# Attention and a SoLU feed-forward layer in one kernel: larger local units, two jobs moved to GpSimd, one to TensorE, and a new instruction order

## The chip, the cores and the metric

The kernel runs on one core of one Trainium2 chip. Five engines matter: TensorE (PE, matmuls), VectorE (DVE), ScalarE (ACT), GpSimd (POOL) and SyncE (SP, which here only issues DMAs). Each executes its own instructions in the order in which they stand in the program, and waits on semaphores for the others. The time is the device time of one execution in microseconds; the lower the better. The kernel before took 507.43 us (median of 3 runs, 505.02 to 507.56).

## The reference

```python
# q, k, v: (8, 8, 576, 64); heads 0-3 see the last 32 keys, heads 4-7 every 32nd key
scores = scale * np.matmul(q, k.transpose(0, 1, 3, 2))
mask_local = (rel >= 0) & (rel < 32)
mask_strided = (rel >= 0) & (pos[None, :] % 32 == pos[:, None] % 32)
attn = softmax(np.where(masks, scores, -1e9))       # eps 1e-9 in the sum
x = np.matmul(attn, v) -> (4608, 512)               # 8 batches of 576 tokens, 8 heads * 64
# feed-forward, on all 4608 tokens
h = x @ w_in                                        # 512 x 1024
solu = h * softmax(h)
ln = (solu - mean) / np.sqrt(var + 1e-6) * g_ln     # over the 1024
out = ln @ w_out                                    # 1024 x 512
```

The input weights arrive as 64-bit floats and are decoded on the chip.

## The kernel before, in words

**Attention.** The scores that a mask keeps are computed in small blocks, and blocks are handled in *units*. `unit(n)` takes unit n; each of the 8 batches has five (`UNITS`): two strided ones (6 and 5 blocks of 54 queries and 54 keys for each of 4 heads) and three local ones (3 blocks each of 64 queries and 96 keys). So units 0 to 4 belong to batch 0 and unit 7 is the first local one of batch 1. A unit runs this chain: the mask is put into the PSUM tile `s_ps` (the first six units by four matmuls of a unit matrix on TensorE, L369; from unit 6 on by a copy on ScalarE, L361, called the *seed*), TensorE adds the fp32 products of queries and keys (L374), VectorE takes the maxima (L380) and subtracts them (L390), ScalarE does the exponentials (L392), VectorE the sums (L393), VectorE two small instructions for the reciprocals (L397, L398), GpSimd the product with them (L401), ScalarE the fp16 high part (L409), VectorE the low part (L410), a DMA transposes both into `pt` (L412), TensorE multiplies with v (L432 strided, L442 local), and ScalarE and VectorE copy the result from PSUM as high and low part (L461, L462) into the rings `xl` and `xs`. In the units of `BY_BLOCK` the exponentials are taken block by block straight from PSUM with their sums (L385). There is one `s_ps`, so a unit's scores can only start when the unit before it has left it.

**v.** For each batch ScalarE squares the raw v (L303, output thrown away into `junk`), a power-of-two scale comes of it, and ScalarE and VectorE split v in high and low parts (L325, L326).

**Feed-forward.** `ff(n)` handles 128 tokens; there are 36. `g1` is 24 matmuls of 128x128 by 128x512 (three fp16 products for each of 4 x 2 pieces, L505 to L507) into two of three PSUM banks `h_ps`; maxima (L511), exponentials (L515), products (L517), centring (L521), squares (L522), the norms on GpSimd (L525 to L555), high and low part of the result (L562, L563), a DMA transpose (L566), and `g2`, again 24 such matmuls (L575 to L577), into `o_ps`; ScalarE scales and stores (L583).

**Weights.** `decode` turns 64-bit floats into 32-bit ones: ScalarE makes the upper bits (L603), VectorE shifts the low word (L606) and joins it (L607). w_in (four pieces) and w_out (four pieces) both pass it, in `prep_w` and `prep_o`. `prep_w` then forms the sum of squares with TensorE (`gram`, L620), and splits w_in (L628 on ScalarE, L629 on VectorE). `prep_o` forms the squares of w_out with ScalarE (L639, eight times) and splits w_out (L651, L652).

**Order.** Every step is entered in a plan with its engine, a planned duration, what it reads and what it writes. `ORDER`, a table of step numbers, gives the order in which they are emitted, and so the order on every engine and on the DMA queue of SyncE. `lock=True` in a step tells the search of that table that a VectorE instruction with two SBUF inputs and a GpSimd instruction exclude each other.

The step that the change replaces in `decode`, and the two reciprocal steps, as they stand before:

```python
nc.vector.tensor_scalar(w0, w0, 29, None, op0=ALU.logical_shift_right)
nc.vector.scalar_tensor_tensor(di, di, 3, w0, op0=ALU.logical_shift_left, op1=ALU.bitwise_or)

nc.vector.tensor_scalar(sm, sm, EPS_SM, 1.0 / P_SCALE, op0=ALU.add, op1=ALU.mult)
nc.vector.reciprocal(sm, sm)
```

Of the kernel before, what the change touches and what calls it, by code (L numbers as in the profile page):

```python
# [753 lines left out]
```

## Time and profile before

| what | value |
|---|---|
| median of 3 runs | 507.43 us (505.02 to 507.56) |
| the profiled execution | 503.42 us, of which the instructions span 501.7 us |
| mean granted TensorE clock | 0.952 |
| busy: PE, DVE, ACT, POOL | 464.5, 353.7, 364.9, 158.3 us |
| first matmul of the first FF | 55.79 us after the span's start |
| PE busy in 200 to 480 us | all of it |

The profile is of one execution. Times in its rows are microseconds from the first instruction, durations of single instructions are in us in the time line and in ns in the groups. A group's row gives line, engine, operation, output<-input, shapes and count, then busy time and mean, then how long the engine stood idle before them and what ended that. Matmuls are pipelined, so a matmul's duration (380 ns for 512 columns) is longer than the distance from one start to the next.

### The profile page before, as it was taken

To read this page: it belongs to the slowest core of one execution; us is meant where nothing else is said; L and a number is where in the kernel's file an instruction comes from. 1 tells how busy PE (TensorE), PEld (TensorE's weight loads), DVE (VectorE), ACT (ScalarE), POOL (GpSimd) and SP (SyncE) were. 2 spreads that over 40 slices of the span, in tenths; PEclk is the share of its full clock that TensorE was granted. 3 is DMA by queue.
4 is the path that set the end of the run, shared out by engine and by line. 5 is a ranking of instruction groups with operands and counts; after the bars stand their busy time and mean duration, and the time that the engine had idled before them with its cause. 6 is when DMAs were issued, how large, how long until landed. Compare 5 with 4: busy or idle time off the path is not lost.

```text
span 501.7 us, 12430 instructions
## 1 busy us (share of the span) xinstructions
PE 464.5 (93%) x5049; PEld 240.7 (48%) x5049; DVE 353.7 (71%) x740; ACT 364.9 (73%) x647; POOL 158.3 (32%) x312
## 2 busy tenths in 40 slices
...
GB/s 316 381 277 338 223 244 168 60 250 231 192 254 115 162 197 204 189 231 159 233 191 209 122 230 170 146 51 197 162 103 96 95 133 171 64 78 101 65 105 105
DMA packets 153817, 88.02 MB, mean 175 GB/s; under 512 B 139808, under 2 KB 140448, under 8 KB 153248
## 3 DMA queue, kind: packets, MB, share of 16 engines
...
q8 instruction: 39, 0.64, 0.5%
q14 instruction: 18, 0.15, 0.1%
...
## 4 chain that ended last, share of the span: by engine, by line
PE 73%; ACT 9%; DVE 7%; DMA 5%; POOL 3%; issue 2%; SPq 1%; ACTq 0%; DVEq 0%; POOLq 0%
PE o_ps L575 11%; PE h_ps L505 10%; PE o_ps L577 10%; PE o_ps L576 10%; PE h_ps L506 10%; PE h_ps L507 10%; PE s_ps L374 6%; DMA cc<-cc 3%; PE x_ps L442 2%; PE x_ps L432 2%; ACT t L385 2%; DMA k<-kstr 1%; DVE m L380 1%; ACT raw L515 1%; DMA raw<-vstr 1%
## 5 line engine op out<-in xcount | busy, mean ns | idle before, releaser
L575 PE MATMUL o_ps<-ohi,cc 128*128 128x512 f16 x272 | 103.4, 380 | 0.9 <-DMA cc<-cc 0.9
L577 PE MATMUL o_ps<-ohi,cc 128*128 128x512 f16 x272 | 103.1, 379 | 0.0
L576 PE MATMUL o_ps<-obuf,cc 128*128 128x512 f16 x272 | 103.1, 379 | 0.0
L401 POOL TENSOR_TENSOR t<-t,m 128x576 f32<-128x576 f32 (+2 forms) x40 | 50.2, 1258 | 89.8 <-DVE m L398 63.7
L511 DVE TENSOR_REDUCE st<-h_ps 128x1 f32<-128x512 f32 x70 | 47.5, 684 | 32.6 <-PE h_ps L507 32.6
L515 ACT ACTIVATE raw<-h_ps,st,vsc 128x512 f32<-128x512 f32 x62 | 47.9, 774 | 20.4 <-DVE st L513 19.4
L563 DVE SCALAR_TENSOR_TENSOR cc<-raw,st,cc 128x1024 f16<-128x1024 f32 (+1 forms) x38 | 46.4, 1224 | 20.9 <-ACT cc L562 20.7
L517 DVE SCALAR_TENSOR_TENSOR raw<-h_ps,raw 128x512 f32<-128x512 f32 x70 | 47.3, 684 | 18.5 <-ACT raw L515 17.9
L505 PE MATMUL h_ps<-w,xl 128*128 128x512 f16 x140 | 53.8, 384 | 0.7 <-DVE raw L517 0.7
L506 PE MATMUL h_ps<-w,xl 128*128 128x512 f16 x140 | 53.4, 381 | 0.0
L507 PE MATMUL h_ps<-w,xl 128*128 128x512 f16 x140 | 53.3, 381 | 0.0
L505 PE MATMUL h_ps<-w,xs 128*128 128x512 f16 x140 | 53.1, 379 | 0.0
L506 PE MATMUL h_ps<-w,xs 128*128 128x512 f16 x140 | 53.1, 379 | 0.0
L507 PE MATMUL h_ps<-w,xs 128*128 128x512 f16 x140 | 53.1, 379 | 0.0
L521 ACT ACTIVATE raw<-raw,st 128x1024 f32<-128x1024 f32 x36 | 41.3, 1148 | 15.6 <-DVE st L520 15.2
L380 DVE TENSOR_REDUCE m<-s_ps 128x6 f32<-128x576 f32 (+2 forms) x40 | 30.4, 761 | 29.0 <-PE s_ps L374 27.9
L562 ACT ACTIVATE cc<-raw,st 128x1024 f16<-128x1024 f32 (+1 forms) x38 | 41.7, 1099 | 11.7 <-POOL st L552 8.9
L374 PE MATMUL s_ps<-k,q 64*54 64x54 f32 (+1 forms) x1280 | 45.7, 286 | 3.4 <-DMA k<-kstr 1.7
L374 PEld LDWEIGHTS s_ps<-k,q 64*54 64x54 f32 (+1 forms) x1280 | 40.0, 201 | 14.4 <-issue 7.1
L577 PEld LDWEIGHTS <-cc 128*128 128x128 f16 x288 | 28.2, 98 | 34.5 <-DMA cc<-cc 0.6
L575 PEld LDWEIGHTS <-cc 128*128 128x128 f16 x288 | 28.1, 98 | 33.5 <-DMA cc<-cc 2.0
L576 PEld LDWEIGHTS <-cc 128*128 128x128 f16 x288 | 28.2, 98 | 29.5
...
## 6 DMA issues: line engine op xcount, KB each, us to landing
...
```

What stands on the lines that cost most here:

```text
L374: nc.tensor.matmul(s_ps[row : row + nq, pair, i * nk : (i + 1) * nk], q_raw[half][hs, q0 : q0 + (nq - 1) * nqb + 1 : nqb], k_raw[half][hs, ...
L401: add("pool", nx * nk / 520 + 0.03, lambda: nc.gpsimd.tensor_tensor(tv, tv, sm.unsqueeze(2).broadcast_to([P, nx, nk]), op=ALU.mult), r=TM, ...
L505: nc.tensor.matmul(hv[i], xhi[cc], whi[:, cc, cols], start=(cc == 0), stop=False)
L506: nc.tensor.matmul(hv[i], xhi[cc], wlo[:, cc, cols], start=False, stop=False)
L507: nc.tensor.matmul(hv[i], xlo[cc], whi[:, cc, cols], start=False, stop=(cc == 3))
L511: add("dve", 0.69, lambda i=i: nc.vector.tensor_reduce((nm, nm2)[i], hv[i], axis=AX.X, op=ALU.max, negate=True), r=[HH[i]], w=[(ST, "nm", i)])
L515: add("act", 0.73, lambda i=i, q=q: nc.scalar.activation(e[:, parts2[i]], hv[i], AF.Exp, bias=nm, scale=hs, accum_out=q), r=[HH[i], (ST, " ...
L517: add("dve", 0.7, lambda i=i, x=x: nc.vector.scalar_tensor_tensor(u[:, parts2[i]], hv[i], 1.0, e[:, parts2[i]], op0=ALU.mult, op1=ALU.mult ...
L563: add("dve", w / 980 + 0.23, lambda cols=cols: nc.vector.scalar_tensor_tensor(c[:, 1, cols], u[:, cols], r, c[:, 0, cols], op0=ALU.mult, o ...
L575: nc.tensor.matmul(o, ct[:, cc, :], ohi[:, cc, :], start=(cc == 0), stop=False)
L576: nc.tensor.matmul(o, ct[:, cc, :], olo[:, cc, :], start=False, stop=False)
L577: nc.tensor.matmul(o, ct[:, 8 + cc, :], ohi[:, cc, :], start=False, stop=(cc == 7))
```

## The change

1. From batch 1 on a batch has two local units, of 5 and 4 blocks, in place of three of 3 (`LATER`); batch 0 keeps its three. There are 33 units in place of 40. Buffers `t`, `p` and `pt` go by the unit's place in the batch, the transposes have 20 and 16 tiles in place of three times 12, and the 5-block unit's product with v uses both PSUM banks of `x_ps`. `BY_BLOCK` has units 2, 3, 4, 7, 8 (36 block columns, as before).
2. All units have their mask seeded by ScalarE; the unit-matrix matmuls go. The strided mask is read as fp32 with a broadcast, so one GpSimd copy less is made.
3. The reciprocals of the softmax sums move from VectorE to GpSimd, as an addition and a power of -1, ahead of GpSimd's product.
4. In `decode` the shifted low word comes from GpSimd (from the top byte of the word, in floating point), and VectorE only joins.
5. The squares of w_out go from ScalarE (eight instructions) to TensorE (`gram`, 32 matmuls of 128 columns into `o_ps`); the product with the squares of g is formed on the sums.
6. The squares of v are written into the v tile that is free, not into `junk`.
7. TensorE's 40 warm-up matmuls of 128 columns become 2 and, later, 10 of 480.
8. The table `ORDER` is a new one; v is fetched first.

```diff
+LATER = [(1, 0, 6), (1, 6, 5), (0, 0, 5), (0, 5, 4)]
-BY_BLOCK = (2, 3, 4, 7, 8, 9)
+BY_BLOCK = (2, 3, 4, 7, 8)
...
+def warm(n, out):
+    for i in range(n):
+        nc.tensor.matmul(out[i % len(out)], ones, ones[:, 0:1].broadcast_to([P, 5 * KL]), start=True, stop=True)
+add("pe", 0.4, lambda: warm(2, [s_ps[:, i, 0 : 5 * KL] for i in range(2)]), r=["ones"], w=[("s", 0), ("s", 1)])
+add("pe", 2.0, lambda: warm(10, [o_ps[:, 0 : 5 * KL]]), r=["ones"], w=["o"])
...
 def unit(n):
-    half, b0, nb = UNITS[j]
+    half, b0, nb = (LATER if b else UNITS)[j]
+    at = j if j < 4 else 2
+    t, m, pb, ptb = t_sb[at], m_sb[n % 5], p_sb[at], pt_sb[at % 2]
...
-    if n >= SEEDED:
-        add("act", nx * nk / 1200 + 0.17, seed, r=["mask"], w=[("s", 0), ("s", 1)])
+    add("act", nx * nk / 1200 + 0.17, lambda: nc.scalar.copy(sv, mk), r=[MK], w=[("s", 0), ("s", 1)])
     def qk():
-        for pair, h, hs, row in heads if n < SEEDED else ():
-            nc.tensor.matmul(s_ps[row : row + D, pair, 0 : nb * nk], unit_sb[hs, hs], mk[hs], start=True, stop=False)
...
-    def recip():
-        nc.vector.tensor_scalar(sm, sm, EPS_SM, 1.0 / P_SCALE, op0=ALU.add, op1=ALU.mult)
-        nc.vector.reciprocal(sm, sm)
-    add("dve", 0.4, recip, r=[M], w=[M], lock=True)
-    add("pool", nx * nk / 520 + 0.03, lambda: nc.gpsimd.tensor_tensor(tv, tv, sm..., op=ALU.mult), r=TM, w=[T])
+    def norm():
+        nc.gpsimd.tensor_scalar(sm, sm, EPS_SM, 1.0 / P_SCALE, op0=ALU.add, op1=ALU.mult)
+        nc.gpsimd.tensor_tensor(sm, sm, minus1.broadcast_to([P, nx]), op=ALU.pow)
+        nc.gpsimd.tensor_tensor(tv, tv, sm.unsqueeze(2).broadcast_to([P, nx, nk]), op=ALU.mult)
+    add("pool", nx * nk / 520 + 1.33, norm, r=[*TM, "minus1"], w=[T, M])
...
-    X = [("x", xb)] if half == 0 else [("x", 0), ("x", 1)]
+    one = half == 0 and nb <= 4
+    X = [("x", xb)] if one else [("x", 0), ("x", 1)]
...
 def decode(dst, src, n, w, room, shift=0):
-    add("dve", 2.02, bits, r=[*RAW, *w], w=[*w, *RAW], lock=True)
+    top = raw.bitcast(U8).rearrange("p f (t b) -> p f t b", b=4)[:, :, 0, 3]
+    add("pool", 1.05, lambda: nc.gpsimd.tensor_scalar(w0, top, -15.5, 1.0 / 32, op0=ALU.add, op1=ALU.mult), r=RAW, w=[("low", n)])
+    add("dve", 1.25, lambda: nc.vector.scalar_tensor_tensor(di, di, 3, w0, op0=ALU.logical_shift_left, op1=ALU.bitwise_or), ...)
...
 def prep_o():
-        for cc in (2 * i, 2 * i + 1):
-            add("act", 0.71, lambda cc=cc: nc.scalar.activation(ob_sb[cc % 2]..., obuf[:, cc], AF.Square, ..., accum_out=o_sc[:, 8 + cc : 9 + cc]), ...)
+        def gram(i=i, dst=dst):
+            x = dst.bitcast(BF16).rearrange("p (f t) -> p f t", t=2)[:, :, 1]
+            for j in range(8):
+                nc.tensor.matmul(o_ps[:, 0:P], x[:, j * P : j * P + P], x[:, j * P : j * P + P], start=(i == 0 and j == 0), stop=(i == 3 and j == 7))
+        add("pe", 0.6, gram, r=OD, w=["o"])
+    add("dve", 0.3, lambda: nc.vector.scalar_tensor_tensor(diag, o_ps[:, 0:P], 1.0, unit_sb, ..., accum_out=o_sc[:, 8:9]), ...)
```

`ORDER` is 51 lines of step numbers, of which no row tells a reader anything. What it does to the engines is shown at two places, both ahead of the first FF.

The first is ScalarE while w_in is split and w_out arrives. Before, three of the four splits of w_in (L628, rows into `w160`) stand ahead of the first decode of w_out (L603, into `obuf0`):

```order
L461 CAST xs0_101<-x0_ps_124 128x3x18x6
L628 ACTIVATE w160_113<-cc0_103,w_sc0_115 128x1024 x2
L409 CAST p2_96<-t2_87 128x6x96
L461 CAST xs0_101<-x1_ps_125 128x2x18x6
L385 ACTIVATE t0_85,m4_93<-s_ps_120,m4_93 128x96 x6
L325 ACTIVATE vs1_73<-vrs0_70,vsc1_78 128x1536
L603 ACTIVATE obuf0_114<-raw0_67 128x1024
L628 ACTIVATE w160_113<-cc0_103,w_sc0_115 128x1024
L361 CAST s_ps_120<-mk_str0_83 128x2x270
```

Now (lines are those of the changed file: L601 decodes, L627 splits w_in, L365 seeds):

```order
L601 ACTIVATE obuf0_114<-raw0_67 128x1024
L408 CAST p30_95<-t30_86 128x6x96
L330 ACTIVATE vs1_72<-vrs0_69,vsc1_77 128x1536
L408 CAST p20_94<-t20_85 128x6x96
L627 ACTIVATE w160_113<-cc0_102,w_sc0_115 128x1024 x4
L459 CAST xs0_100<-x0_ps_124 128x3x18x6
L385 ACTIVATE t20_85,m4_91<-s_ps_120,m4_91 128x96 x6
L365 COPY s_ps_120<-mask0_80 128x2x324
L459 CAST xs0_100<-x1_ps_125 128x2x18x6
L601 ACTIVATE obuf0_114<-raw0_67 128x1024
L365 COPY s_ps_120<-mask0_80 128x2x270
```

The first decode of w_out has moved ahead of all four splits of w_in, of the exponentials of unit 4 and of the seeds of units 5 to 7.

The second place is VectorE over the decoding of w_in (`cc0`). Before:

```order
L606 TENSOR_SCALAR raw0_67<-raw0_67 128x1024
L607 SCALAR_TENSOR_TENSOR cc0_103<-cc0_103,raw0_67 128x1024
L606 TENSOR_SCALAR raw0_67<-raw0_67 128x1024
L607 SCALAR_TENSOR_TENSOR cc0_103<-cc0_103,raw0_67 128x1024
L380 TENSOR_REDUCE m3_92<-s_ps_120 128x6
L410 TENSOR_TENSOR p1_95<-t1_86,p1_95 128x2x5x54
L397 TENSOR_SCALAR m2_91<-m2_91 128x6
L398 RECIPROCAL m2_91<-m2_91 128x6
```

Now:

```order
L607 SCALAR_TENSOR_TENSOR cc0_102<-cc0_102,raw0_67 128x1024
L380 TENSOR_REDUCE m3_90<-s_ps_120 128x6
L387 TENSOR_SCALAR m3_90<-m3_90 128x6
L409 TENSOR_TENSOR p10_93<-t10_84,p10_93 128x2x5x54
L607 SCALAR_TENSOR_TENSOR cc0_102<-cc0_102,raw0_67 128x1024 x2
```

The shifts (L606) and the reciprocals (L397, L398) are gone from VectorE; GpSimd has them in the same stretch, in this order:

```order
L606 TENSOR_SCALAR raw0_67<-raw0_67 128x1024
L397 TENSOR_SCALAR m1_88<-m1_88 128x10
L398 TENSOR_TENSOR m1_88<-m1_88,minus10_111 128x10
L399 TENSOR_TENSOR t10_84<-t10_84,m1_88 128x540
L606 TENSOR_SCALAR raw0_67<-raw0_67 128x1024
```

GpSimd's normalisation of a unit (L397 to L399) now stands behind a shift that waits for a piece of w_in. The first FF still follows the scores of unit 7, which now has 5 blocks.

More of the change, by code (lines that the diff above doesn't have):

```diff
@@ L11 @@
 I32 = mybir.dt.int32
+U8 = mybir.dt.uint8
 AF = mybir.ActivationFunctionType
@@ L196, in attn_solu_kernel @@
     (nhalf,) = buf("nhalf", [P, 1])
+    (minus1,) = buf("minus1", [P, 1])
     (ones,) = buf("ones", [P, P], BF16)
@@ L220, in attn_solu_kernel @@
     add("dve", 0.2, init, w=["nhalf"])
+    add("pool", 0.1, lambda: nc.gpsimd.memset(minus1, -1.0), w=["minus1"])
     add("dve", 0.3, lambda: nc.vector.memset(ones, 1.0), w=["ones"])
-    def warm():
-        for _ in range(40):
-            nc.tensor.matmul(o_ps[:, 0:P], ones, ones, start=True, stop=True)
-    add("pe", 2.13, warm, r=["ones"], w=["o"])
+    def warm(n, out):
[3 more added lines that the diff above has]
+    add("pe", 2.0, lambda: warm(10, [o_ps[:, 0 : 5 * KL]]), r=["ones"], w=["o"])
+    add("dve", 0.1, lambda: nc.vector.memset(s_ps[:, 1, 504:512], 0.0), w=[("s", 1)])
     def masks_bf16():
         m = mask_sb
-        nc.gpsimd.tensor_copy(mk_str, m[:, 2:3, 0:QS].broadcast_to([P, 6, QS]))
         nc.gpsimd.tensor_copy(mk_loc[:, 0, 0:1], m[:, 0:1])
-        nc.gpsimd.tensor_copy(mk_loc[:, 0, 1:3], m[:, 1:2].broadcast_to([P, 2, KL]))
-        nc.gpsimd.tensor_copy(mk_loc[:, 1], m[:, 1:2].broadcast_to([P, 3, KL]))
+        nc.gpsimd.tensor_copy(mk_loc[:, 0, 1:5], m[:, 1:2].broadcast_to([P, 4, KL]))
+        nc.gpsimd.tensor_copy(mk_loc[:, 1], m[:, 1:2].broadcast_to([P, 5, KL]))
     def load_masks():
         add("sp", 0.4, lambda: nc.sync.dma_start(mask_sb, masks), w=["mask_raw"])
-        add("pool", 1.34, masks_bf16, r=["mask_raw"], w=["mask"])
-    for i in range(NPB):
+        add("pool", 1.4, masks_bf16, r=["mask_raw"], w=["mask"])
+    for i in range(4):
         def pads(i=i):
-            nc.gpsimd.memset(p_sb[i][:, :, QS:D], 0.0)
-            nc.gpsimd.memset(p_sb[i][:, :, D if i == 1 else KL : P], 0.0)
-        add("pool", 0.56, pads, w=[("p", i)])
+            if i < 2:
+                nc.gpsimd.memset(p_sb[i][:, :, QS:D], 0.0)
+            nc.gpsimd.memset(p_sb[i][:, :, (KL, D)[i == 1] : P], 0.0)
+        add("pool", (0.56, 0.9, 0.6, 0.5)[i], pads, w=[("p", i)])
     def unit_matrix():
@@ L253, in attn_solu_kernel, with pow2_scale @@
     add("dve", 0.05, lambda: nc.vector.memset(k_raw[0][:, 0:KPAD], 0.0), w=["kpad"])
-    def pow2_scale(dst, parts, r, w, room, top=14, mul=1.0, square=None, adds=False, shift=SQ, floor=2.0**-40):
+    def pow2_scale(dst, parts, r, w, room, top=14, mul=1.0, square=None, adds=False, shift=SQ, floor=2.0**-40, product=False):
         tot, T = room
@@ L262, in total @@
             for i, part in enumerate(parts):
-                nc.tensor.matmul(tot, ones, part.bitcast(BF16)[:, 1:2], start=(i == 0 and not adds), stop=(i == len(parts) - 1), skip_group_check=adds)
+                one = product or not (i or adds)
+                nc.tensor.matmul(tot[:, i : i + 1] if product else tot, ones, part.bitcast(BF16)[:, 1:2], start=one, stop=product or i == len(parts) - 1, skip_group_check=adds)
         add("pe", 0.06 * len(parts) + 0.05, total, r=["ones", *r], w=[T])
         def root():
-            nc.vector.tensor_scalar(dst[:, 0:1].bitcast(I32), tot.bitcast(I32), 1, 0x7F800000, op0=ALU.logical_shift_right, op1=ALU.bitwise_and)
+            low = tot
+            if product:
+                low = dst[:, 0:1]
+                nc.vector.tensor_scalar(low, tot[:, 0:1], tot[:, 1:2], None, op0=ALU.mult)
+            nc.vector.tensor_scalar(dst[:, 0:1].bitcast(I32), low.bitcast(I32), 1, 0x7F800000, op0=ALU.logical_shift_right, op1=ALU.bitwise_and)
         def fn():
@@ L355, in unit @@
         t4 = tv.rearrange("p (c x) k -> p c x k", c=2)
-        mk = (mk_loc[:, 0 if b0 == 0 else 1] if half == 0 else mk_str[:, 0:nb]).rearrange("p x k -> p (x k)")
-        if n >= SEEDED:
-            def seed():
-                nc.scalar.copy(s_ps[:, :, 0 : nb * nk], mk.unsqueeze(1).broadcast_to([P, 2, nb * nk]))
-            add("act", nx * nk / 1200 + 0.17, seed, r=["mask"], w=[("s", 0), ("s", 1)])
+        if half:
+            mk, MK = mask_sb[:, 2:3, 0:QS].unsqueeze(1).broadcast_to([P, 2, nb, QS]), "mask_raw"
+        else:
+            mk, MK = mk_loc[:, 0 if b0 == 0 else 1, 0:nb].unsqueeze(1).broadcast_to([P, 2, nb, KL]), "mask"
+        add("act", nx * nk / 1200 + 0.17, lambda: nc.scalar.copy(sv, mk), r=[MK], w=[("s", 0), ("s", 1)])
         def qk():
             heads = [(pair, h, slice(h * D, h * D + D), (h ^ pair) * D) for pair in range(2) for h in range(2)]
-            for pair, h, hs, row in heads if n < SEEDED else ():
-                nc.tensor.matmul(s_ps[row : row + D, pair, 0 : nb * nk], unit_sb[hs, hs], mk[hs], start=True, stop=False)
             for i in range(nb):
@@ L374, in qk @@
                     nc.tensor.matmul(s_ps[row : row + nq, pair, i * nk : (i + 1) * nk], q_raw[half][hs, q0 : q0 + (nq - 1) * nqb + 1 : nqb],
-                                     k_raw[half][hs, k0 : k0 + nk], start=False, stop=(i == nb - 1), skip_group_check=n >= SEEDED)
-        add("pe", nb * 0.231 + (0.25, 0.09)[half] - (0.2 if n >= SEEDED else 0.0), qk, r=[("q", half), ("k", half), "mask", "unit", "kpad"], w=[("s", 0), ("s", 1)])
+                                     k_raw[half][hs, k0 : k0 + nk], start=False, stop=(i == nb - 1), skip_group_check=True)
+        add("pe", nb * 0.231 + (0.25, 0.09)[half] - 0.2, qk, r=[("q", half), ("k", half), "kpad"], w=[("s", 0), ("s", 1)])
         SS = [("s", 0), ("s", 1)]
@@ L449, in unit @@
             q0, w = off + QL * b0, QL * nb
-            src = [x_ps[xb][:, 0 : 2 * w].rearrange("p (c q) -> p c q", c=2)]
-            dst = [[x[:, :, q0 : q0 + w] for x in xl]]
+            src = [x_ps[xb][:, 0 : 2 * w].rearrange("p (c q) -> p c q", c=2)] if one else [x[:, 0:w] for x in x_ps]
+            dst = [[x[:, :, q0 : q0 + w] for x in xl]] if one else [[x[:, c, q0 : q0 + w] for x in xl] for c in range(2)]
             ring = [("xl", q0 // QL + i) for i in range(nb)]
```

86 lines of the change are left out of this document (33 added, 53 removed), and 80 rows, old and new, of the table ORDER.

## The prediction

> **What bounds the kernel now.** I read the page's head first, then the busy times by stage, then TensorE's time line where it begins to be busy without a break.
>
> ```profile
> span 501.7 us, 12430 instructions
> PE 464.5 (93%) x5049; PEld 240.7 (48%) x5049; DVE 353.7 (71%) x740; ACT 364.9 (73%) x647; POOL 158.3 (32%) x312
> ```
>
> TensorE leads with 93%, but an average says nothing of where its 37 us of idle time lie. The stages do (busy us of each engine, TensorE's clock, DMA share, GB/s):
>
> ```profile
> 0.00:10.00 10.00, 6.39 (x92) 5.74 (x93) 0.98 (x4) 2.05 (x2) 3.85 (x16) 0.99 0.80 290
> 10.00:20.00 10.00, 3.14 (x74) 2.52 (x73) 8.83 (x19) 8.41 (x14) 2.77 (x2) 0.50 1.02 425
> 20.00:30.00 10.00, 5.54 (x124) 4.46 (x124) 9.55 (x14) 8.75 (x30) 0.00 (x0) 0.50 1.12 303
> 40.00:50.00 10.00, 3.18 (x101) 2.86 (x96) 9.37 (x9) 4.76 (x6) 1.15 (x1) 0.50 1.16 342
> 60.00:70.00 10.00, 9.30 (x76) 4.53 (x70) 8.53 (x25) 9.75 (x27) 1.09 (x1) 1.00 0.81 244
> 240.00:280.00 40.00, 40.00 (x497) 20.52 (x499) 30.59 (x68) 29.59 (x51) 14.77 (x27) 1.00 0.88 194
> ```
>
> From 60 us on TensorE is full (the row of 240 to 280 stands for all of 160 to 490). Before that it is idle for more than half of the time at half clock, VectorE is at 8.8 to 9.6 of 10, ScalarE nearly as high, and the DMA engines have a share of 1.0 to 1.2. So there are two kernels in one: a start of 56 us that ends with the first FF, set by VectorE, ScalarE and DMA together, and 446 us of matmuls behind it (501.7 less 55.79), which only fewer or shorter matmuls make shorter. This is how the start ends:
>
> ```profile
> 54.61 1.25 PE L374 MATMUL s_ps<-k,q 64*64 64x96 f32 x24 [0.96 <-DMA q<-qloc]
> 55.79 0.61 PE L505 MATMUL h_ps<-w,xl 128*128 128x512 f16 x1
> 57.95 0.38 PE L505 MATMUL h_ps<-w,xs 128*128 128x512 f16 x1
> 58.17 0.38 PE L506 MATMUL h_ps<-w,xs 128*128 128x512 f16 x1
> 55.38 0.56 DVE L462 TENSOR_TENSOR xl<-x_ps,xl 128x384 f16<-128x384 f32 x1
> ```
>
> The scores of unit 7 wait for their queries until 54.61, the first FF follows at 55.79, and its last operand, the low part of `xl`, is written from 55.38 to 55.94. Two chains thus end within a microsecond: the fetches, and VectorE's.
>
> **Part 1: what VectorE is relieved of before the first FF.**
>
> ```profile
> L606 DVE TENSOR_SCALAR raw<-raw 128x1024 int32<-128x1024 int32 x7 | 4.8, 685 | 0.0
> 20.82 0.68 DVE L606 TENSOR_SCALAR raw<-raw 128x1024 int32<-128x1024 int32 x1
> 21.60 1.23 DVE L607 SCALAR_TENSOR_TENSOR cc<-cc,raw 128x1024 int32<-128x1024 int32 x1
> L397 DVE TENSOR_SCALAR m<-m 128x6 f32<-128x6 f32 x24 | 4.7, 195 | 0.1
> L398 DVE RECIPROCAL m<-m 128x6 f32<-128x6 f32 x24 | 4.6, 191 | 0.8
> ```
>
> A shift takes 0.78 us from its start to the join's (20.82 to 21.60). Four of w_in and three of w_out run before 55.94 (7 x 0.78 = 5.5 us), and six pairs of reciprocals (6 x 0.39 = 2.3 us). VectorE thus loses 7.8 us of the work ahead of the first FF. That is the most the first FF can come earlier by VectorE alone; the least is 0, if the fetches hold it.
>
> **Part 2: the fetches.** The new order fetches v first, then keys and queries, but ahead of unit 7's queries stand the same things as before: all of w_in, three pieces of w_out, two batches of v, keys and queries, and four transposes. The DMA engines' busy tenths from 20 to 35 and from 35 to 50 us, in 40 slices each:
>
> ```profile
> DMA  9989889983799799996969992008999998996898
> ...
> DMA  6994499999899999979989999999999999999999
> ```
>
> Taking a 9 as full, the first row lacks about 6 slices of 0.375 us, the second 2: together 3.1 us in which the DMA engines had nothing to do, because a transpose or a fetch waited for VectorE. With VectorE ahead these are what can be won: the first FF comes between 0 and 3.1 us earlier. Neither end is favoured by a row, so I take half and round up: **-1.7 us**. The 56 us of the start then become 54.
>
> **Part 3: TensorE's own work behind the first FF.**
>
> ```profile
> 138.79 1.48 PE L374 MATMUL s_ps<-k,q 64*54 64x54 f32 x48
> 140.20 0.39 PE L505 MATMUL h_ps<-w,xl 128*128 128x512 f16 x1
> 243.99 1.25 PE L374 MATMUL s_ps<-k,q 64*54 64x54 f32 x40
> 245.18 0.39 PE L505 MATMUL h_ps<-w,xl 128*128 128x512 f16 x1
> 221.13 0.38 PE L505 MATMUL h_ps<-w,xs 128*128 128x512 f16 x1
> 221.87 0.28 PE L442 MATMUL x_ps<-pt,ve 96*64 96x64 f16 x6
> 221.99 0.26 PE L442 MATMUL x_ps<-pt,vl 96*64 96x64 f16 x6
> 222.58 0.95 PE L374 MATMUL s_ps<-k,q 64*64 64x96 f32 x24
> L620 PE MATMUL h_ps<-cc 128*128 128x128 bf16 x32 | 4.1, 305 | 3.3 <-DVE cc L607 3.3
> ```
>
> The matmuls per block stay; what goes is the cost of entering a unit. Scores: 6 blocks hold TensorE 1.41 us (138.79 to 140.20), 5 blocks 1.19, so a block costs 0.22 and 0.09 is left; the entry costs another 0.09, since three FF matmuls of 0.216 after 221.13 end at 221.78 and the unit begins at 221.87. Together 0.18. Product with v: 0.71 us from 221.87 to 222.58 for 36 matmuls, of which a group of 6 takes about 0.1 (0.12 the first), so 0.11 is left, plus 0.09 of entry: 0.20. Seven batches lose one local unit: 7 x 0.38 = 2.7 us; the least is 0, if the fixed part hides in something else.
>
> Against it stand the grams of w_out. Two of the four run behind the first FF, 16 matmuls; w_in's 32 took 4.1 us at half clock, so at full clock 16 take 4.1 x 0.5 x 0.5 = 1.0 us. The eight small sums of squares before (0.2 us) become two. Sum +0.8. The first two grams stand between the scores of units 6 and 7, where TensorE waits for the seed anyway, and cost nothing unless the seed is early (then 2 us). The unit-matrix matmuls (L369) and the warm-up lie in TensorE's idle time: 0. Unit 7's two extra blocks leave the full part (0.5) and lengthen the start (0.5 at half clock): 0. **Part 3: -1.9 us.**
>
> **Part 4: what moves onto engines that were not the bound.**
>
> ```profile
> L361 ACT CAST s_ps<-mk_loc 128x576 f32<-128x576 bf16 x21 | 13.5, 642 | 6.2 <-DVE t L390 3.1 <-PE o_ps L577 2.3 <-ACT ob L583 0.4
> L639 ACT ACTIVATE ob<-obuf 128x512 bf16<-128x512 f32 x8 | 5.0, 627 | 3.9 <-DVE obuf L607 3.8
> L552 POOL TENSOR_TENSOR st<-st,nhalf 128x2 f32<-128x2 f32 x32 | 23.0, 718 | 2.7
> L231 POOL CAST mk_str<-mask 128x324 bf16<-128x324 f32 x1 | 0.5, 456 | 1.9 <-DMA mask<-masks 1.9
> L232 POOL CAST mk_loc<-mask 128x96 bf16<-128x96 f32 x1 | 0.3, 270 | 0.0
> ```
>
> ScalarE: six seeds more (6 x 0.64 = 3.9 us), eight squares less (5.0 and their readouts, 0.19 each, 6.5 us). It comes out 2.6 us lighter in the start, though the seeds come early and the squares went late. GpSimd: a shift costs 1.03 us by the copies (0.186 us for 228 elements more, on 1024), eight of them 8.2 us; a power on 12 elements is not shown, by L552 it is at least 0.72 us for two, and if every further pair cost as much, 4.3; I take 1.0, as one-element and two-element powers differ little, plus 0.3 for the addition. 33 units x 1.3 = 43 us. GpSimd goes from 158 to some 210 of 500 us, no bound; the latency of a unit grows by 1 us, behind which the full part has always had matmuls ready. 0, with up to +2.7 if it takes back what part 3 gives.
>
> Sum: -1.7 - 1.9 = **-3.6 us**: the span goes from 501.7 to 498.1, and with the 1.7 us around it the profiled execution from 503.42 to 499.8. That execution lay 4 us under the median of the runs, 507.43; taken off that, **503.8 us**.
>
> **A rule weighed.** By the Trainium skill (TensorE: Matmul & The Clock Gate, The HAM clock gate), TensorE runs at half clock until it has been busy for some 3.4 us. The trace agrees: clock 0.50 up to the first FF, whose first six matmuls take 2.16 us (55.79 to 57.95) and later ones 0.22 each. By that rule the two grams just ahead of unit 7 could open the clock before the first FF, and the sum would be about 0.9 us lower, -4.5.
>
> **The rivals.**
>
> *VectorE's relief goes through.* If the fetches keep up, the first FF comes 7.8 us earlier: -7.8 - 1.9, 497.7. For it: VectorE is the fullest engine of the start. Against it, the DMA share over 1.0 for forty microseconds, and these rows:
>
> ```profile
> 19.09 1.80 DVE L326 SCALAR_TENSOR_TENSOR vs<-vrs,vsc,vs 128x1536 f16<-128x1536 f32 x1
> 40.00 1.15 POOL L401 TENSOR_TENSOR t<-t,m 128x576 f32<-128x576 f32 x1 [7.02 <-DVE m L398]
> 40.38 2.38 DVE L326 SCALAR_TENSOR_TENSOR vs<-vrs,vsc,vs 128x1536 f16<-128x1536 f32 x1 [0.55 <-ACT vs L325]
> ```
>
> The same VectorE instruction takes 0.58 us more beside GpSimd's product. Seven shifts of 1.03 us beside VectorE's joins can give back up to 7 of the 7.8 us. The Trainium skill (GPSIMD Engine Reference, Specifications) has this as a rule: GpSimd shares its SBUF interfaces with VectorE, and VectorE instructions with two SBUF inputs contend for them. The join is one.
>
> *ScalarE takes over.* It is at 9.75 of 10 from 60 to 70 us; if its chain of exponentials holds the second and third FF, an earlier first FF is waited off. Then only part 3 counts: 505.5.
>
> *The longer units stall the full part.* If part 3 is lost, -1.7 + 0.8: 506.5.
>
> *Slower: ScalarE waits for w_out.* In the new order the first decode of w_out stands ahead of all four splits of w_in, the exponentials of unit 4 and three seeds.
>
> ```profile
> 41.70 1.13 ACT L603 ACTIVATE obuf<-raw 128x1024 f32<-128x1024 f32 x1 [1.35 <-DMA raw<-w_out]
> L628 ACT ACTIVATE w<-cc,w_sc 128x1024 f16<-128x1024 f32 x4 | 4.5, 1142 | 0.0
> 38.74 1.61 ACT L325 ACTIVATE vs<-vrs,vsc 128x1536 f16<-128x1536 f32 x1
> ```
>
> Before, w_out landed at 41.70. If it does so again, ScalarE then has its decode, a split of v and two casts (4 us), the four splits (4.5) and unit 4's exponentials and a seed (2.5): 52.7. Three units' scores follow through the one `s_ps`, some 3 us each (scores 1.2, maxima and subtraction 1.4, seed 0.6): the first FF at 61.5, +5.7 - 1.9, 511.2. It decides from a landing at about 40 us on; I expect 34 to 37, an estimate: its room is free once w_in's third piece is joined, near 28 us if the first is at 21.60 as before, and its megabyte (2.5 us at the 425 GB/s of 10 to 20 us) queues behind a transpose and a batch's queries.
>
> **How the numbers follow.** Half a per cent, 2.5 us, is about what a measurement can tell from no change. Chances: the forecast 0.40 (own range 501 to 506), relief going through 0.15, ScalarE 0.20, stalls 0.12, slower 0.13. Range 496 to 510.5. Faster (under 504.9): the forecast's most, 0.34, the first rival, and a third of ScalarE's case: 0.57. Slower: the last, 0.13. The same: the rest, 0.30.
>
> **What would show it.** The first FF at 54 us (47.5 for the first rival, 61 for the last); no shift or reciprocal on VectorE; GpSimd near 210 us; 160 to 490 us still full. Wrong would be: idle time on TensorE among the first three FFs (ScalarE), or behind 100 us (longer units), or a first decode of w_out that waits beyond 40 us.

## The result, and the profile after

The changed kernel took 517.90 us (median of 4 runs, 516.27 to 519.22), the kernel before 506.23 (median of 4, 504.51 to 507.56): a ratio of 1.0251, 95% interval 1.0223 to 1.0278. It is slower by 2.5%; the forecast was 503.8 with a range of 496 to 510.5. The profiled execution took 519.22 us with a span of 517.5, that of before 503.42 with 501.7. The spans thus differ by 15.8 us and the medians by 11.7, because the profiled execution of before lay 2.8 us under its median and that of after 1.3 over.

The head of the page and the first two lines of the chain that ended last, of the changed kernel:

```profile
span 517.5 us, 12281 instructions
PE 466.0 (90%) x5023; PEld 240.3 (46%) x5023; DVE 343.1 (66%) x629; ACT 360.0 (70%) x617; POOL 251.2 (49%) x379
...
PE 63%; POOL 10%; DVE 8%; ACT 8%; DMA 5%; issue 4%; SPq 1%; ACTq 0%; DVEq 0%; POOLq 0%
PE h_ps L503 9%; PE h_ps L504 9%; PE h_ps L505 9%; PE o_ps L573 9%; PE o_ps L574 8%; PE o_ps L575 8%; PE s_ps L374 5%; POOL m L398 4%; POOL t L399 3%; DMA raw<-w_in 2%; PE x_ps L440 2%; DMA cc<-cc 2%; DVE cc L561 1%; PE x_ps L430 1%; DVE raw L515 1%
```

TensorE is busy as long as before (466.0 against 464.5 us) and has 51.5 us of idle time instead of 37. VectorE lost 10.6 us, GpSimd gained 92.9, and GpSimd now carries 10% of the chain; the power, L398, is its largest part. The groups of GpSimd, shapes kept apart (busy us, mean ns of one):

```profile
L398 POOL TENSOR_TENSOR m<-m,minus 128x10 f32<-128x10 f32 x15 | 30.2, 2013 | 1.2
L398 POOL TENSOR_TENSOR m<-m,minus 128x12 f32<-128x12 f32 x8 | 18.3, 2283 | 0.7
L398 POOL TENSOR_TENSOR m<-m,minus 128x8 f32<-128x8 f32 x7 | 11.6, 1651 | 0.6
L398 POOL TENSOR_TENSOR m<-m,minus 128x6 f32<-128x6 f32 x3 | 4.0, 1320 | 0.3
L606 POOL TENSOR_SCALAR raw<-raw 128x1024 int32<-128x1024 uint8 x7 | 8.7, 1245 | 12.8 <-DMA raw<-w_out 9.1 <-DMA raw<-w_in 3.4
```

A power costs 1.32 us for 6 elements and 2.28 for 12, about 0.16 us an element: 64 us in 33 units, where the forecast had 33. Where TensorE then stands still, in its time line (start, us, instruction, idle time ahead of it and what ended it):

```profile
45.86 1.50 PE L374 MATMUL s_ps<-k,q 64*54 64x54 f32 x48 [8.38 <-ACT s_ps L365]
52.73 0.88 PE L374 MATMUL s_ps<-k,q 64*54 64x54 f32 x24 [1.32 <-issue]
58.15 0.61 PE L503 MATMUL h_ps<-w,xl 128*128 128x512 f16 x1
77.49 0.38 PE L503 MATMUL h_ps<-w,xl 128*128 128x512 f16 x1 [2.56 <-DVE raw L515]
101.29 0.28 PE L440 MATMUL x_ps<-pt,ve 96*64 96x64 f16 x6 [3.65 <-issue]
213.15 0.19 PE L264 MATMUL s_ps<-vm,ones 128*128 128x1 bf16 x2 [1.81 <-ACT vs L308]
387.85 0.28 PE L440 MATMUL x_ps<-pt,vl 96*64 96x64 f16 x6 [2.04 <-DVE xl L460]
```

The first FF begins at 58.15 us (before 55.79). Behind it lie 459.35 us (before 445.9), and all visible pauses of TensorE there add up to 13.7 us (before 3.2). The releasers named are ScalarE and VectorE; the engine behind the last of them is GpSimd. Four stages of three to five microseconds (busy us of PE, PEld, DVE, ACT, POOL, then the clock, DMA share, GB/s) and, around 385 us, three engines' time lines say it:

```profile
78.03:81.44 3.41, 3.41 (x10) 1.21 (x8) 3.06 (x5) 3.41 (x7) 0.00 (x0) 0.50 0.15 29
100.00:105.00 5.00, 3.71 (x27) 1.62 (x27) 1.63 (x4) 3.20 (x8) 0.01 (x1) 0.69 1.25 213
380.00:385.00 5.00, 5.00 (x55) 2.49 (x48) 0.92 (x1) 0.50 (x2) 4.73 (x4) 1.00 0.68 108
390.00:395.00 5.00, 5.00 (x13) 1.67 (x12) 1.72 (x6) 4.59 (x6) 0.84 (x3) 0.50 0.14 52
```

```profile
376.05 2.26 POOL L398 TENSOR_TENSOR m<-m,minus 128x12 f32<-128x12 f32 x1
378.40 1.27 POOL L399 TENSOR_TENSOR t<-t,m 128x648 f32<-128x648 f32 x1
379.75 1.23 POOL L397 TENSOR_SCALAR m<-m 128x10 f32<-128x10 f32 x1
381.07 1.95 POOL L398 TENSOR_TENSOR m<-m,minus 128x10 f32<-128x10 f32 x1
383.10 1.79 POOL L399 TENSOR_TENSOR t<-t,m 128x960 f32<-128x960 f32 x1
384.92 0.99 ACT L408 CAST p<-t 128x960 f16<-128x960 f32 x1 [4.40 <-POOL t L399]
387.31 0.49 DVE L460 TENSOR_TENSOR xl<-x_ps,xl 128x320 f16<-128x320 f32 x1 [6.38 <-ACT xl L459]
```

From 380 to 385 us GpSimd is busy for 4.73 of 5 and ScalarE for 0.50: two units' norms stand in a row on GpSimd, ScalarE waits 4.40 us for the product in order to cast it, the copy of `x_ps` behind that cast on ScalarE comes late, VectorE waits 6.38 for the copy, and TensorE 2.04 for VectorE. (The power is not all of that delay: the addition at 379.75 took 1.23 us, where the mean of its form is 0.37.) Then it costs once more, at half clock: from 388.6 to 395.5 us, from 101.9 to 105.3 behind the pause of 3.65 us, and from 78.0 to 81.4 behind the pause of 2.56 the trace has the clock at 0.50, and the matmuls of 128 x 512 follow each other at twice the distance. With half of TensorE's busy time in such stretches as the estimate of what they cost, these three lose 3.1, 1.7 and 1.7 us, and the start of the first FF 1.4 (before 0.9).

So the 13.45 us that the part behind the first FF is longer are made up of pauses (+10.6), half clock (+7.0 by this estimate) and, as what is left, TensorE's own work (-4.2). What is left is alike in all the profiles: 433.9 to 434.6 us in the eleven of the new order, 437.8 to 438.5 in the three of the old one (up to the last matmul).

Two causes offered themselves for the pauses: the power, and for those marked "issue", where no semaphore is named, the arrival of TensorE's own instructions. A third was the new order itself with its larger units.

### The profile page after: what moved, and what is told of

It is laid out like the page before. It is cut to its first block, busy times and chain, and to the rows that moved or that the text cites. A ratio compares the mean times of both kernels' runs of the same rounds, so it can differ in the third digit from the quotient of the medians.

```text
span 517.5 us, 12281 instructions
## 1 busy us (share of the span) xinstructions
PE 466.0 (90%) x5023; PEld 240.3 (46%) x5023; DVE 343.1 (66%) x629; ACT 360.0 (70%) x617; POOL 251.2 (49%) x379
## 4 chain that ended last, share of the span: by engine, by line
PE 63%; POOL 10%; DVE 8%; ACT 8%; DMA 5%; issue 4%; SPq 1%; ACTq 0%; DVEq 0%; POOLq 0%
PE h_ps L503 9%; PE h_ps L504 9%; PE h_ps L505 9%; PE o_ps L573 9%; PE o_ps L574 8%; PE o_ps L575 8%; PE s_ps L374 5%; POOL m L398 4%; POOL t L399 3%; DMA raw<-w_in 2%; PE x_ps L440 2%; DMA cc<-cc 2%; DVE cc L561 1%; PE x_ps L430 1%; DVE raw L515 1%
## 5 line engine op out<-in xcount | busy, mean ns | idle before, releaser
L374 PE MATMUL s_ps<-k,q 64*54 64x54 f32 (+1 forms) x1280 | 44.5, 287 | 24.1 <-ACT s_ps L365 21.2
L561 DVE SCALAR_TENSOR_TENSOR cc<-raw,st,cc 128x1024 f16<-128x1024 f32 (+1 forms) x38 | 48.0, 1267 | 27.0 <-ACT cc L560 26.6
L398 POOL TENSOR_TENSOR m<-m,minus 128x10 f32<-128x10 f32 (+3 forms) x33 | 64.0, 1939 | 2.7
L503 PE MATMUL h_ps<-w,xl 128*128 128x512 f16 x140 | 54.7, 390 | 4.1 <-DVE raw L515 4.1
L504 PE MATMUL h_ps<-w,xl 128*128 128x512 f16 x140 | 54.5, 390 | 0.0
L505 PE MATMUL h_ps<-w,xl 128*128 128x512 f16 x140 | 54.5, 389 | 0.0
L503 PE MATMUL h_ps<-w,xs 128*128 128x512 f16 x140 | 54.2, 387 | 0.0
L504 PE MATMUL h_ps<-w,xs 128*128 128x512 f16 x140 | 53.9, 385 | 0.0
L505 PE MATMUL h_ps<-w,xs 128*128 128x512 f16 x140 | 53.8, 384 | 0.0
L548 POOL TENSOR_SCALAR st<-st 128x1 f32<-128x1 f32 x32 | 7.2, 226 | 86.7 <-ACT raw L520 86.0
L399 POOL TENSOR_TENSOR t<-t,m 128x648 f32<-128x648 f32 (+4 forms) x33 | 46.9, 1422 | 2.6
L575 PEld LDWEIGHTS <-cc 128*128 128x128 f16 x288 | 28.3, 98 | 35.4 <-DMA cc<-cc 1.2
L573 PEld LDWEIGHTS <-cc 128*128 128x128 f16 x288 | 28.3, 98 | 33.8 <-DMA cc<-cc 0.8
```

Source lines behind the costliest of these rows:

```text
L374: nc.tensor.matmul(s_ps[row : row + nq, pair, i * nk : (i + 1) * nk], q_raw[half][hs, q0 : q0 + (nq - 1) * nqb + 1 : nqb], k_raw[half][hs, ...
L398: nc.gpsimd.tensor_tensor(sm, sm, minus1.broadcast_to([P, nx]), op=ALU.pow)
L399: nc.gpsimd.tensor_tensor(tv, tv, sm.unsqueeze(2).broadcast_to([P, nx, nk]), op=ALU.mult)
L503: nc.tensor.matmul(hv[i], xhi[cc], whi[:, cc, cols], start=(cc == 0), stop=False)
L504: nc.tensor.matmul(hv[i], xhi[cc], wlo[:, cc, cols], start=False, stop=False)
L505: nc.tensor.matmul(hv[i], xlo[cc], whi[:, cc, cols], start=False, stop=(cc == 3))
```

## The experiments

**1. Take the power away.** The kernel without it, and the kernel with the reciprocals on VectorE again; then the shift on VectorE again, and both.

```diff
 e1        nc.gpsimd.tensor_scalar(sm, sm, EPS_SM, 1.0 / P_SCALE, ...)
-          nc.gpsimd.tensor_tensor(sm, sm, minus1.broadcast_to([P, nx]), op=ALU.pow)
 e2
-          nc.gpsimd.tensor_scalar(sm, ...); nc.gpsimd.tensor_tensor(sm, ..., op=ALU.pow)
+          nc.vector.tensor_scalar(sm, ...); nc.vector.reciprocal(sm, sm)
 e3
-          nc.gpsimd.tensor_scalar(w0, top, -15.5, 1.0 / 32, op0=ALU.add, op1=ALU.mult)
+          nc.vector.tensor_scalar(w0, w0, 29, None, op0=ALU.logical_shift_right)
 e4        the edits of e2 and e3
```

> The changed kernel with the power left out: GpSimd still adds, scales and multiplies, but by the softmax sum instead of its reciprocal (that part of the computation is left out). GpSimd is relieved of 33 powers, 64.0 us by the trace of the changed kernel, and nothing is put on another engine. Theory P (the price of the power: 1.94 us a unit where the order had left room for 1.33 with the addition; late products delay the casts of p, then VectorE and TensorE, and each pause of TensorE is followed by some us at half clock): 500 to 507 us, most of the visible idle time of TensorE behind the first FF (13.7 us) goes. Theory L (the shift of the low weight bits on GpSimd, which waits in order for the fetch of w_out with a norm behind it): 514 or more. Theory O (the new order and the 5- and 4-block units by themselves): 514 or more.

> The changed kernel with addition and reciprocal on VectorE again (33 pairs, 0.39 us each by the trace before, 12.9 us), at the norm's place in the new order; GpSimd keeps the product and the shift. Theory P: 503 to 509 us, GpSimd near 177 us busy. Theory L: 514 or more. Theory O: 514 or more.

> The changed kernel with the shift of the low weight bits on VectorE again (8 of 0.78 us by the trace before), at its place in the new order; the power stays on GpSimd. Theory P: 516 to 521 us, since only the start is touched. Theory L: 510 or less, the first FF before 56 us. Theory O: 515 to 520.

> Both on VectorE again: what is left of the change is the new order, the 5- and 4-block units and the squares of w_out on TensorE. Theory P: 503 to 510 us. Theory L: 510 or less. Theory O: 513 or more; a time under 506 would say that the rest of the change is worth something by itself.

| kernel | median us | ratio to before (95%) | span of the profile | first FF | behind it |
|---|---|---|---|---|---|
| before (with these four) | 505.11 | 1 | 501.7 | 55.79 | 445.9 |
| changed | 517.90 | 1.0251 (1.0223 to 1.0278) | 517.5 | 58.15 | 459.4 |
| e1, no power | 505.29 | 0.9991 (0.9965 to 1.0016) | 504.1 | 56.49 | 447.6 |
| e2, reciprocals on VectorE | 507.28 | 1.0047 (1.0029 to 1.0065) | 505.7 | 57.23 | 448.5 |
| e3, shift on VectorE | 518.42 | 1.0273 (1.0230 to 1.0316) | 516.6 | 60.16 | 456.4 |
| e4, both on VectorE | 507.05 | 1.0040 (1.0015 to 1.0066) | 505.6 | 57.91 | 447.7 |

(The row "before" has the span of the profile shown above.) Theory P holds: the power costs 12.6 us if nothing replaces it, 10.6 if VectorE does the work. Theory L falls: without the shift on GpSimd the time is the same. Theory O falls by its number (513 or more), but leaves a question: e4 has neither job on GpSimd and is still no faster than before. The first two rows below are the stage of 350 to 400 us in the changed kernel and in e1; then the time line of TensorE in e2:

```profile
350.00:400.00 50.00, 47.26 (x422) 22.94 (x421) 28.75 (x51) 33.29 (x53) 31.36 (x40) 0.93 0.53 101
...
350.00:400.00 50.00, 50.00 (x427) 24.13 (x425) 34.15 (x60) 34.58 (x53) 20.62 (x41) 1.00 0.55 108
```

```profile
93.73 0.29 PE L440 MATMUL x_ps<-pt,vl 96*64 96x64 f16 x6
93.82 0.29 PE L440 MATMUL x_ps<-pt,ve 96*64 96x64 f16 x6
93.92 0.29 PE L440 MATMUL x_ps<-pt,vl 96*64 96x64 f16 x6
94.01 0.38 PE L440 MATMUL x_ps<-pt,ve 96*64 96x64 f16 x12
94.20 0.29 PE L440 MATMUL x_ps<-pt,vl 96*64 96x64 f16 x6
98.24 0.37 PE L440 MATMUL x_ps<-pt,ve 96*64 96x64 f16 x6 [3.75 <-issue]
```

Without the power TensorE is full in 350 to 400 us, the pauses at 213 and 388 us are gone, and the one of 2.56 at 77 us is 0.97 in e1 and 1.05 in e2. One pause stays in all four: the one with no semaphore, 2.94, 3.75, 2.57 and 3.39 us long, always ahead of the same matmul, in the middle of a product with v. The DMA queues and issues of e2 from 90 to 98 us:

```profile
DMA packets 2015, 2.43 MB, mean 304 GB/s; under 512 B 1525, under 2 KB 1525, under 8 KB 2012
q1 hardware_dynamic: 1895, 2.17, 93.6%
q8 instruction: 1, 0.02, 0.8%
q14 instruction: 2, 0.02, 0.5%
vrl<-vloc SPq DMA_DIRECT2D x1, 640.0 KB, 8.5
k<-kloc SPq DMA_DIRECT2D x1, 576.0 KB, 4.5
q<-qloc SPq DMA_DIRECT2D x1, 576.0 KB, 6.9
```

The instructions have DMA queues of their own (q8, q14), and in this window they share the DMA engines with 1.8 MB of q, k and v that the new order issues in one go. The single packet of q8 in this window can be placed more closely. It is a block of 16 KB; there is none of q8 from 94.40 to 95.88 us, and one starts between 95.88 and 96.00:

```profile
q1 hardware_dynamic: 112, 0.47, 93.9%
q14 instruction: 1, 0.01, 1.3%
...
q8 instruction: 1, 0.02, 54.0%
```

TensorE stands still from 94.49; the block is on its way from 95.89 to 96.93, and TensorE goes on at 98.24, 1.31 us behind its landing. In all eleven profiles of the new order the matmul behind this stop starts 1.3 to 1.7 us behind the landing of the same block, the seventh of q8. So this "issue" is a wait for instructions.

**2. Move these three fetches, or make them small.** In e5 three numbers of the order are moved; e9 leaves the order and fetches one eighth of the columns, so part of the q, k and v of these batches is left out. e6 adds two moves in the start.

```diff
 e5 (on e2): SyncE's steps 481, 480, 503 (k, q, v) come behind 336 (a transposition of p)
 e6 (on e5): VectorE's 44 (scale of w_in) behind 43; ScalarE's 147 (decode of w_out) behind 51
 e9 (on e2):
+        if b == 2 and not half:
+            w //= 8
         load(1.49, q_raw[half][:, 0:w], (qloc, qstr)[half][b][:, 0:w], [("q", half)])
 ...     (k likewise; v of b == 3 likewise)
```

> The kernel with the reciprocals on VectorE in the new order (507.28 us), and its three fetches of the local q, k and v of the third batch (1.8 MB) issued behind the next transposition of p, near 100 us instead of 90 to 92. The stop of TensorE at 94.5 us for 3.75 us lies in the middle of a run of small matmuls, with no semaphore named and with the DMA engines busy by 0.9 to 1.1. Theory F (TensorE's instructions come by DMA and stood behind these fetches): the stop goes, with the half clock behind it (98 to 103 us): 501 to 503.5 us, and a stop may come elsewhere in small. Rival D (160 small matmuls in 3 us use instructions up faster than they come, whatever else the DMA does): the stop stays within 1 us, 506 to 508.5 us.

> As the run with the three fetches moved, and two steps of the start moved too: VectorE makes the scale of w_in directly behind its sum (not behind a maximum and a low part of p, 2.3 us later), and ScalarE decodes the first quarter of w_out behind the four splits of w_in instead of ahead of a cast of p. Theory S (the start is long because ScalarE and VectorE do things in the wrong order between 33 and 46 us, 7.99 us of idle TensorE at 44.39): the first FF at 55 to 56.5 us instead of 57.23, the time 0.7 to 2 us under the run without this edit. Rival (fetches and the stops of TensorE's instructions set the first FF): the first FF at 57 to 58 us, the time within 0.7 us of it.

> The kernel with the reciprocals on VectorE in the new order (507.28 us), with the three fetches (local q and k of the third batch, local v of the fourth) in their place at 90 to 92 us but one eighth of their columns each (0.2 instead of 1.8 MB); the rest of these tiles keeps the data of an earlier batch, so that part of the computation uses other numbers. Theory F (the bytes of these fetches hold up TensorE's instructions): the stop near 95 us shrinks below 1.5 us, 501 to 503.5 us. Rival (not the bytes but the place in the queue, or the dense matmuls): the stop stays at 2.5 us or more, 506 to 508.5 us.

| kernel | median us | ratio to before (95%) | span | first FF | behind it | the stop |
|---|---|---|---|---|---|---|
| e5, fetches moved | 501.97 | 0.9942 (0.9924 to 0.9959) | 500.4 | 55.78 | 444.6 | 0.96 |
| e6, and the start reordered | 502.40 | 0.9942 (0.9924 to 0.9960) | 501.2 | 56.39 | 444.8 | 0.92 |
| e9, fetches one eighth | 502.89 | 0.9968 (0.9937 to 0.9998) | 501.0 | 57.05 | 444.0 | 1.16 |

(The v that is moved is the fourth batch's, not the third's, as the first of these expectations has it.) Theory F holds by both ways: with the bytes elsewhere, or away, the block of q8 lands at 92.87 (e5) and 94.42 us (e9) instead of 96.93, the stop falls from 3.75 to about 1 us, and the half clock behind it goes. The stage of 80 to 110 us in e2 and in e5, and the stop in e5:

```profile
80.00:110.00 30.00, 25.27 (x389) 13.49 (x386) 20.74 (x47) 22.55 (x51) 12.25 (x23) 0.89 0.78 168
...
80.00:110.00 30.00, 27.12 (x453) 15.65 (x442) 24.33 (x54) 25.87 (x55) 12.90 (x24) 1.00 0.89 198
94.57 0.28 PE L440 MATMUL x_ps<-pt,ve 96*64 96x64 f16 x6 [0.96 <-issue]
```

What remains, about 1 us at the same matmul, speaks for a part of rival D: some 150 small matmuls in 3 us use instructions up, and the next block is not ready in time. The Trainium skill (Runtime: NRT & Kernel Launch, Instruction fetch mechanics) says that an engine fetches its instructions in blocks by a DMA queue of its own while it executes, and that this is mostly hidden. The trace agrees with the queue, and not with the hiding: 3.75 us were in the open here, and 0.96 with the three fetches elsewhere (the DMA engines' share was 0.94 from 88 to 91 us in e5, and 0.40 from 91 to 93, when the block came).

Theory S falls: the two moves brought the decode of w_out behind the splits and the scale of w_in 1.9 us forward (34.97 against 36.86 in e2), and the first FF came no earlier than in e5: at 56.39, which is within theory S's 55 to 56.5, but e5 has 55.78 without the moves, and the time is the same. ScalarE's time line in e6 offers a reason:

```profile
33.85 0.68 ACT L408 CAST p<-t 128x576 f16<-128x576 f32 x1
34.42 1.58 ACT L330 ACTIVATE vs<-vrs,vsc 128x1536 f16<-128x1536 f32 x1
35.90 0.66 ACT L408 CAST p<-t 128x576 f16<-128x576 f32 x1
36.46 4.26 ACT L627 ACTIVATE w<-cc,w_sc 128x1024 f16<-128x1024 f32 x4
40.63 1.12 ACT L601 ACTIVATE obuf<-raw 128x1024 f32<-128x1024 f32 x1
...
44.03 0.70 ACT L365 COPY s_ps<-mask 128x648 f32<-128x648 f32 x1
```

ScalarE works without a pause up to the seed of unit 5 at 44.03 (43.71 in e5), in either order. That less work on ScalarE would bring the first FF forward was not tried. e5 is the version that beats both kernels: 0.58% under the kernel before, 3.1% under the changed one.

**3. One part alone in the kernel before.** e7 puts addition and power on GpSimd there, e8 the shift.

```diff
 e7
-            nc.vector.tensor_scalar(sm, sm, EPS_SM, 1.0 / P_SCALE, op0=ALU.add, op1=ALU.mult)
-            nc.vector.reciprocal(sm, sm)
+            nc.gpsimd.tensor_scalar(sm, sm, EPS_SM, 1.0 / P_SCALE, op0=ALU.add, op1=ALU.mult)
+            nc.gpsimd.tensor_tensor(sm, sm, minus1.broadcast_to([P, nx]), op=ALU.pow)
 e8
-            nc.vector.tensor_scalar(w0, w0, 29, None, op0=ALU.logical_shift_right)
+            nc.gpsimd.tensor_scalar(w0, top, -15.5, 1.0 / 32, op0=ALU.add, op1=ALU.mult)
```

> The kernel before, with one part of the change alone: addition and reciprocal of the softmax sums on GpSimd (tensor_scalar and power) in place of VectorE, old order, old units, shift on VectorE. Theory P (the power by itself costs, 1.94 us a unit in the way of every product): 511 to 519 us, with idle TensorE behind 100 us that the kernel before does not have. Rival N (it hurts only in the new order, which counted 1.33 us for it and has it on its chain): 504 to 508 us.

> The kernel before, with the shift of the low weight bits alone on GpSimd, at its place ahead of VectorE's next operation on the same data. My forecast's first step (VectorE relieved of 8 x 0.78 us, 5.5 us of it ahead of the first FF, fetches the next bound): the first FF 0 to 3 us earlier, 502 to 505 us. Rival (GpSimd's 1.1 to 1.25 us is longer than VectorE's 0.78 and VectorE waits for it in place, since the order gives no room): the first FF 0 to 3 us later, 505 to 508 us.

e7 took 514.29 us (ratio 1.0180, 1.0140 to 1.0220), e8 506.73 (1.0028, 1.0007 to 1.0049). So the power costs 9 us in the old order too, and rival N falls: it is not the new order or its longer units that make it dear. In e7's profile the first FF comes at 58.99, 3.2 us later than before, and the pauses behind it add up to 8.8 us, against 3.2. But the old order was made for 0.4 us on VectorE, and the new one counted 1.30 for addition and power: both counted less than it takes, so whether an order made with the true price would hide the power is not shown. Three pauses in e7, whose counterparts are missing in the profile of before:

```profile
131.26 0.95 PE L376 MATMUL s_ps<-k,q 64*64 64x96 f32 x24 [1.75 <-ACT s_ps L363]
230.74 0.95 PE L376 MATMUL s_ps<-k,q 64*64 64x96 f32 x24 [1.81 <-ACT s_ps L363]
254.16 1.30 PE L376 MATMUL s_ps<-k,q 64*54 64x54 f32 x40 [1.92 <-ACT s_ps L363]
```

In e8 the first FF came 0.27 us earlier (55.52), at the lower end of the forecast's 0 to 3.1, and the whole was slightly slower: the forecast's expectation missed the time, the rival's the place.

**4. Do the two costs add, and is the shift worth anything?**

```diff
 e10 = the changed kernel with the order of e5 (481, 480, 503 behind 336)
 e11 = e5 with the shift on VectorE (the edit of e3)
 e12 = the changed kernel with the short fetches of e9
```

> The changed kernel itself, power on GpSimd, with only the three fetches issued behind the next transposition of p, as in the run that had the reciprocals on VectorE. Theory P with F (the two costs add: the power some 11 us, the stop at 101 us with its half clock some 5): 511.5 to 514 us. Rival (the power delays the products so that the time of the stop is waited for anyway): 516 to 518.5 us.

> The best version so far (new order, reciprocals on VectorE, three fetches moved, 501.97 us) with the shift of the low weight bits on VectorE again too, at its place in the order. If GpSimd's shift is worth what my forecast took for it (5.5 us of VectorE ahead of the first FF, 1.7 us of the end): 503.5 to 505 us, the first FF 1.5 to 3 us later than 55.78. Rival (worth nothing that can be measured, as the old order with the shift alone on GpSimd said): 501 to 503 us.

> The changed kernel itself, power on GpSimd, with the three fetches in their place but one eighth of their columns each (the rest of these tiles keeps an earlier batch's data, so that part of the computation uses other numbers). The run with these fetches moved left two levels (513.1 and 514.3, 517.6 and 517.7 us), so whether the two costs add is open. If they add: 511 to 514.5 us, the stop of 3.65 us under 1.8. Rival (the power's delays take the place of the stop): 516 to 518.5 us.

e10 took 515.93 us in the median, but its four runs lie on two levels (513.05 and 514.27, 517.60 and 517.69), one near each theory; why there are two is open. Its profile is of the lower one, with a span of 511.3 and a stop of 1.62. e12 took 514.74 (513.94 to 516.65; ratio 1.0183, 1.0159 to 1.0208), which is under the changed kernel beyond both intervals and just over the range of "they add": 3.2 us came back, where the same edit gave 4.4 from e2 to e9. So they add for the most part. In e12's profile the issue pause in the scores of unit 6, which is 1.32 in the changed kernel and 1.20 in e2, is 1.96; it too ends 1.2 us behind the landing of a 16 KB block of q8.

```profile
53.05 0.89 PE L377 MATMUL s_ps<-k,q 64*54 64x54 f32 x24 [1.96 <-issue]
```

e11 took 503.74 (0.9981, 0.9952 to 1.0009), which is within the first expectation by its time; the first FF, at 56.99, came 1.2 us later than in e5 and not 1.5 to 3. The interval overlaps e5's, and e3 and e4 showed no difference: what the shift on GpSimd is worth lies between 0 and 1.8 us and is not settled.

## Why the prediction was wrong, point by point

*Where the miss lies.* By the profiles the forecast was 499.8 and the result 519.22: 4.15 us too little for the start and 15.3 for the part behind it. Of these 15.3, e2 takes back 10.9 with the reciprocals on VectorE, and e5 another 3.9 with the fetches moved.

*Part 1 (VectorE relieved of 7.8 us).* Shifts and reciprocals went as forecast, but other work came in their place: ahead of the first FF VectorE was busy 39.66 us in the changed kernel and 43.26 before, 3.6 less. The worth was small. In profiles without an issue pause over 0.4 us in unit 6, the first FF came at 55.78 (e5) and 56.39 (e6) with the shift on GpSimd and at 56.99 (e11) and 57.91 (e4) with it on VectorE, so in the new order the shift buys 0.6 to 2.1 us of the start, by single profiles; in the old one 0.27.

*Part 2 (first FF at 54).* It failed by 4.15 us. (The 3.1 us of its DMA row are a slip: 8 slices of 0.375 us are 3.0.) I read from two chains that met within a microsecond that the fetches and VectorE alone end the start; but ScalarE is busy for 10.98 of the 11 us from 34 to 45 (9.04 before), and TensorE's longest wait there, 8.38 us, ends with ScalarE's seed. Its list that I drew up for the slower rival (decode, split of v, casts, four splits, exponentials, seed: 11 us) is that work: in the changed kernel it ran from 34.91 to the seed at 45.10. I had made it depend on w_out landing late. w_out landed early, as I expected, and the chain took its time all the same. That it is this chain that sets the start is read from the time lines; no run has made it shorter. At best (e5) the start is as long as before. The changed kernel's 58.15 is that plus 1.32 of instruction pause plus what the power delays (e2 against the changed kernel: 0.9).

*Part 3 (-1.9 behind the first FF).* The way was right, the size was met by luck. With the power and the fetches out of the way the part behind the first FF takes 444.6 (e5), 444.0 (e9) and 443.5 (e11) against 445.9, so -1.3 to -2.4. But TensorE's own work fell by about 4 us (434.0 to 434.3 against 438.2), twice the term, and pauses of 4.7 to 5.5 us against 3.2 took much of it back. What makes the work shorter by more than the saved entries is open. So it is luck too that the forecast's -3.6 is close to the -3.2 of e5, which is another kernel than the one forecast.

*Part 4 (GpSimd no bound, 0 to +2.7).* This step failed, and it is the largest part of the miss. I bounded the power by 0.72 to 4.3 us from a row with two elements and took 1.0; it is 1.94 in the mean (2.28 for the 12 elements that the bounds were for), and grows by 0.16 us an element, which one row of two elements could not tell. The larger fault is the sentence that hid it: "behind which the full part has always had matmuls ready". That was read from a full TensorE, and a full TensorE does not say by how much its next operands are early. The slack of a microsecond was not there at every place: a late product delays ScalarE's next cast, all that stands behind that cast on ScalarE, and so TensorE. That a quarter or half of an engine's time is free says nothing of its latency in a chain; GpSimd was busy 49% and on the path. In place of 0 to +2.7 the runs show 10.6 us (e2) to 12.6 (e1) for the power in the new order, and 9 in the old one.

*The clock rule.* I applied it to the first FF, where it changed nothing (its first matmuls were again at half clock; only in e4 and e11 did the first FF run at full clock from its start). And the clock of before was at 0.50 from 10 us on, not from the start: the row of 0 to 10 us has 0.99. The rule mattered elsewhere: the three pauses of 2 us and more in the full part were each followed by 3.4 to 6.8 us at half clock (6.5 us lost in all, by the estimate above), and the one of 1.81 was not. The Trainium skill (TensorE: Matmul & The Clock Gate, The HAM clock gate) names about 3.4 us of idle time for that; the trace shows it behind 3.65 us, but also behind 2.56, and at 387.85, where 2.04 us of pause, eight groups of six small products and another 0.70 lie together. In e7 it followed a pause of 1.92 us and not those of 1.75 and 1.81. So here less than 3.4 us was enough.

*What was missing altogether.* The new order's three fetches in a row (1.8 MB, issued at 90 to 92 us in e2) stood in the order that I read, and I looked at them only as data. That TensorE's instructions travel the same way was in none of my terms: 4.4 to 5.3 us of the loss with the reciprocals on VectorE, about 3 with the power.

*The rivals.* "The longer units stall the full part" named the right place (idle TensorE behind 100 us) with the wrong cause, and put it at 2.7 us where the pauses alone came to 10.6. None had GpSimd as the bound.
